# Reordering pair 0's second-half scores, two exponentials and the last output rows in a fused attention and feed-forward kernel

## The chip, the cores and the metric

The kernel runs on one core of a Trainium2 chip. The metric is device time in microseconds (us). Before the change five runs gave a median of 241.13 us (241.03 to 241.76).

## The reference

Two blocks follow each other. The first is windowed attention over `q, k, v` of shape (4 batches, 8 heads, 768 rows, 64 columns); each query sees the first 8 keys and its last 96 keys, and a slope per head times the distance is subtracted from the score:

```python
scores = scale * q @ k.T - slope[h] * dist      # masked outside the window
a = exp(scores - max) ; a = a / (sum(a) + 1e-9)
x = (a @ v)            # laid out as 3072 tokens x 512
```

The second is a gated feed-forward block with a hidden width of 1536:

```python
g = x @ w_gate
out = ((g * sigmoid(g)) * (x @ w_val)) @ w_out   # 3072 x 512, float32
```

## The kernel before

**Tiles.** The 3072 tokens are cut into 8 tiles of 384; tile 0 is the first half of batch 0, tile 1 its second half, and so on. For each tile the hidden width is cut into 12 slices of 128. One slice is a gate product (4 matmuls of 384 columns into the PSUM tile `gps`), a value product (4 matmuls into `vps`), a tanh on ScalarE (`th`, L564), a combination on VectorE (`sl`, L569) and a multiplication on VectorE (`hT`, L573), which is the activated slice in 16 bits. A block of 128 output rows is 12 matmuls of 512 columns into `ops` (L585), an evacuation on ScalarE (`osb`, L591) and a write by SyncE's DMA queue (L592). The very last block of 128 rows has its own function, `out_last`.

**Attention around it.** Heads are worked in four pairs per batch. For batch 0 the two halves of 384 rows are worked apart. A pair's second half needs: transposes of its keys and queries on TensorE (`turn_half`, L298, into `trs`), copies of these out of PSUM into `kT` (three copies of 96, 240 and 48 columns, L319) and into `qT` (one copy of 384 columns, L336), a bias product that writes slope times distance (`bias`, L345, into four `sc` banks), the scores that add to it (`scores_half`, L356), and exponentials on ScalarE (L367): two of 264 columns for which = 0 and two of 432 columns for which = 1. Denominators and numerators follow (L445).

**PSUM.** There are eight banks with fixed names. `a0` to `a3` go round for scores, bias and numerators; the first four gates of tile 0 stand in them too. `o0` holds an output block, or transposes. `x0`, `x1`, `x2` go round for the gates and values (`spare`), so that each of these waits for the reader of the one three places before it. Gate 4 stands in `x1`, gate 5 in `x2`, value 4 in `x0`, value 5 in `x1`, gate 6 in `x2`: gate 6 can start when gate 5 has been read by its `sl`.

**Order.** Nothing is scheduled automatically; every engine works its instructions in the order in which the code emits them, so the order of the calls is the order on each engine, and semaphores alone hold an engine back. For tile 0 this order is the list `tile0` (L802). A pair (f, 0) is gate f, (f, 1) is value f; other entries are attention steps. The gates 0 to 3 are multiplied ahead of the list, and `first_val(0)`, `first_val(1)` multiply the first two of four terms of values 0 and 1, so that (0, 1) and (1, 1) multiply the last two terms. `trh(h0, h1, ...)` turns and copies two pairs, `bias_of(0, w)` and `scores_of(0)` are pair 0's bias and scores, and `sch(hp)` is bias and scores of another pair in one step.

A list `later` holds work that is put off: `scores_half` with `put_off` appends its two exponentials of 432 columns to it instead of emitting them. The loop over `tile0` (L865) calls `run_later(1)`, which takes one entry, ahead of each gate or value except (8, 1):

```python
if item != (8, 1):
    run_later(1)
gate_or_val(0, f, which, ...)      # products, then tanh and sl, or hT
```

So an entry that is waiting is emitted on ScalarE ahead of the tanh of the gate that takes it.

**The DMA queues** of GpSimd bring the weights, the next batch's keys, queries and values in the meantime; the issues are in program order too, and their place is the same before and after. SyncE's queue writes outputs; of the last block, one half is written from SyncE's queue and the other from ScalarE's.

Of the kernel before, what the change touches and what calls it, by code (L numbers as in the profile page):

```python
# [37 lines left out]
def kernel(  # L38
# [12 lines left out]
    nc = tc.nc  # L51
# [7 lines left out]
    DM = H * D  # L59
# [5 lines left out]
    TB = 384  # L65
# [174 lines left out]
    def spare(name, dt=FP32):  # L240
        tag = state["x"][gv.get("n", 0) % len(state["x"])]
        gv["n"] = gv.get("n", 0) + 1
        return single(name, tag, dt)

    def single(name, tag, dt=FP32):
        return ps.tile([128, 512 if dt == FP32 else 1024], dt, name=name, tag=tag)
# [8 lines left out]
    def run_later(n):  # L255
        for _ in range(n):
            if later:
                later.pop(0)()
# [285 lines left out]
    def products(t, f, which, c0, c1, dst=None):  # L544
        if f == 0 and which == 0 and c0 == 0:
            hTs[t] = sb2.tile([128, NFF, TB], FP16, name="hT", tag="hT", bufs=3)
        if c0 == 0:
            if dst is None:
                dst = spare("gv"[which] + "ps")
            gv[f, which] = dst  # L550
        w = (wg, wv)[which]
        for c in range(c0, c1):
            nc.tensor.matmul(  # L553
                gv[f, which][:, 0:TB], lhsT=w[:, c, 128 * f:128 * f + 128],
                rhs=x_of(t)[:, c, :],
                start=(c == 0), stop=(c == NC - 1))

    def gate_or_val(t, f, which, c0=0):
        products(t, f, which, c0, NC)
        dst = gv.pop((f, which))  # L560

        if which == 0:
            th = sb2.tile([128, TB], FP32, name="th", tag="th")
            nc.scalar.activation(out=th, in_=dst[:, 0:TB], func=AF.Tanh, scale=0.5)  # L564
            if t == 0 and f < 4:
                sl = sb2.tile([128, TB], FP32, name="sl", tag="ns", bufs=4)
            else:
                sl = sb2.tile([128, TB], FP32, name="sl", tag="sl")
            nc.vector.scalar_tensor_tensor(  # L569
                out=sl, in0=th, scalar=1.0, in1=dst[:, 0:TB], op0=AluOp.add, op1=AluOp.mult)  # L570
            gv["sl", f] = sl
        else:
            nc.vector.tensor_mul(hTs[t][:, f, :], dst[:, 0:TB], gv.pop(("sl", f)))  # L573
# [18 lines left out]
            nc.sync.dma_start(out=out[r0:r0 + 128, :], in_=osb)  # L592

    def out_last(t, i):
        r0, n = TB * t + 128 * i, DM // 2
        for side, (ev, dq) in enumerate(((nc.vector.tensor_scalar_mul, nc.sync),
                                         (nc.scalar.mul, nc.scalar))):
            ops = single("ops", f"a{i + side}")
            c0 = n * side
            for f in range(NFF):  # L600
                nc.tensor.matmul(  # L601
                    ops[:, 0:n], lhsT=hTs[t][:, f, 128 * i:128 * i + 128],
                    rhs=wo[:, f, c0:c0 + n], start=(f == 0), stop=(f == NFF - 1))
            osb = sb2.tile([128, n], FP32, name="osb", tag="th")
            ev(osb, ops[:, 0:n], 0.5)
            dq.dma_start(out=out[r0:r0 + 128, c0:c0 + n], in_=osb)

    NT = TOK // TB
    pairs = {(b, hp): Pair(b, hp) for b in range(B) for hp in range(NP)}
# [30 lines left out]
    V, A = nc.vector.tensor_copy, nc.scalar.copy  # L640
# [64 lines left out]
    def first_gates(*terms):  # L705
        for c, f in terms:
            products(0, f, 0, c, c + 1, hb[f])
# [20 lines left out]
    def vas(b, half):  # L728
        return lambda: both_values(b, half)
# [1 line left out]
    def tr(b, hp):  # L731
        return pairs[b, hp].transposes

    def trh(h0, h1, last):
        def step():
            b0, b1 = single("trs", "o0", FP16), spare("trs", FP16)
            (a, b), (c, d) = [(t[:, 0:TB], t[:, TB:2 * TB]) for t in (b0, b1)]
            pair_of = [(h0, (c, a)), (h1, (d, b))]
            for hp, tr in pair_of:
                pairs[0, hp].turn_half(1, tr)  # L740
            for hp, tr in pair_of:
                pairs[0, hp].copy_half(1, tr, V, A if hp == h0 else last)
        return step

    def sch(hp):
        def step():
            p = pairs[0, hp]
            scs = [p.bias(1, 0), p.bias(1, 1)]
            for which in range(2):
                p.scores_half(1, which, scs[which], which == 1 and hp != 1)  # L750
        return step
# [32 lines left out]
    def bias_of(hp, which):  # L784
        def step():
            pairs[0, hp].sc[1, which] = pairs[0, hp].bias(1, which)
        return step

    def scores_of(hp):
        def step():  # L790
            for which in range(2):
                pairs[0, hp].scores_half(1, which, pairs[0, hp].sc[1, which], which == 1)
        return step

    def first_val(f):
        return lambda: products(0, f, 1, 0, 2)
# [2 lines left out]
    V(out=dist[:, 2 * WIN + 168:], in_=dist[:, WIN:WIN + 48])  # L799
    first_gates(*[(c, f) for f in range(4) for c in range(2)])  # L800
    first_gates((2, 0), (2, 1), (2, 2), (3, 0), (3, 1), (2, 3), (3, 2), (3, 3))
    tile0 = [(0, 0), (1, 0), (2, 0), (3, 0), trh(0, 1, A), first_val(0), first_val(1),  # L802
             bias_of(0, 0), bias_of(0, 1), (0, 1), (1, 1), scores_of(0), (2, 1),
             trh(2, 3, V), sch(1), (3, 1), (4, 0), sch(2), (5, 0), (4, 1), (5, 1),
             (6, 0), (6, 1), sch(3), (7, 0), (7, 1), (8, 0), vas(0, 1), (8, 1)]

    def ff(t, f0, f1, n_out=(0,)):
# [22 lines left out]
    for b, base, rate, v_at in ((2, 20, 2.0, (31, 32, 33, 34, 35, 36, 37)), (3, 38, 1.4, (56, 57, 58, 59, 60, 61, 62))):  # L830
        items = [(base, lambda b=b: stage_rows(b)), (base + 1, lambda b=b: load_ends(b))]
        n = 0
# [27 lines left out]
    def take(step_list):  # L860
        run_later(len(later))
        for step in step_list:
            step()

    for item in tile0:  # L865
        if callable(item):
            take([item])
            continue
        f, which = item
        if item != (8, 1):  # L870
            run_later(1)
        gate_or_val(0, f, which, (NC if f < 4 else 0, 2 if f < 2 else 0)[which])
        for fn in after.pop((0, f, which), []):
            fn()
# [22 lines left out]
    for i in range(2):  # L897
        for part in range(4):
            out_part(NT - 1, i, part)
    out_last(NT - 1, 2)  # L900


# [33 lines left out]
```

## Time and profile before

The profile shows one execution, which took 241.76 us; its span, from the first to the last instruction, is 240.0 us, so 1.76 us lie around the span.

| what | value |
|---|---|
| median of 5 runs | 241.13 us |
| profiled execution | 241.76 us |
| its span | 240.0 us |
| TensorE (PE) busy | 233.1 us, 97% |
| VectorE (DVE) busy | 167.4 us, 70% |
| ScalarE (ACT) busy | 127.6 us, 53% |
| GpSimd (POOL) busy | 94.0 us, 39% |
| granted TensorE clock | 1.000 |
| four matmuls of 384 columns, in the chain | 0.65 us |
| the last block's 24 matmuls, in the chain | 2.63 us |

A row of the timeline has the start in us from the span's start, the length in us, the engine, the line of the code, the operation, what it writes and reads, the shapes and a count, for several merged instructions of the same kind; in brackets stands idle time of the engine ahead of it and what ended it. The end of a matmul is modelled, so a matmul's row lasts longer than the step to the next one; the step is read from the starts. PEld is the loading of weights, which goes on beside PE.

### The profile page before, as it was taken

The numbers are of one execution on the slowest core, as the hardware profiler recorded it, in microseconds if no ns is written. First come the engines' busy times: TensorE is split into PE (matmuls) and PEld (weight loads), VectorE is DVE, ScalarE is ACT, GpSimd is POOL, SyncE is SP. The second block draws the span as 40 slices with busy tenths as digits, with TensorE's granted clock in tenths as the row PEclk, the third lists the DMA queues.
The fourth block names the chain that finished last, engine by engine and source line by source line (L and its number), as shares of the span: only waits on it lengthen the run. The fifth ranks groups of instructions, "written<-read, shape, count | busy, mean of one in ns | idle before, by whom it ended". The sixth has DMA issues, their size and how long they took to land.

```text
span 240.0 us, 6040 instructions
## 1 busy us (share of the span) xinstructions
PE 233.1 (97%) x2424; PEld 135.6 (57%) x2424; DVE 167.4 (70%) x365; ACT 127.6 (53%) x288; POOL 94.0 (39%) x113
## 2 busy tenths in 40 slices
PE   7799999999999999999999999999999999999994
PEld 4555565656555556555655556555655556555543
DVE  6689559978897678776785668776785668555520
ACT  4747675888856365376356365376356435233311
POOL 8986673668970002994072152700031213000000
PEclk9999999999999999999999999999999999999999
DMA  7999999999998537999139849930110110111022
GB/s 134 158 200 201 181 203 205 196 165 159 156 137 125 122 82 120 117 131 122 44 62 109 117 109 133 120 61 0 48 44 3 44 44 3 46 45 44 12 79 87
DMA packets 83332, 25.00 MB, mean 104 GB/s; under 512 B 72600, under 2 KB 80360, under 8 KB 83304
## 3 DMA queue, kind: packets, MB, share of 16 engines
q0 software_dynamic: 64208, 14.05, 64.0%
q1 hardware_dynamic: 18664, 10.29, 17.7%
q8 instruction: 19, 0.31, 0.5%
q10 hardware_dynamic: 432, 0.27, 0.4%
q14 instruction: 9, 0.07, 0.1%
HBM read 28.62 MB, written 6.29 MB: 145 GB/s over the span
## 4 chain that ended last, share of the span: by engine, by line
PE 91%; ACT 3%; DVE 2%; DMA 2%; issue 1%; POOL 0%; DVEq 0%; ACTq 0%; POOLq 0%
PE gps L553 26%; PE vps L553 26%; PE ops L585 25%; PE num L445 4%; PE sc L385 3%; PE den L445 2%; DMA q<-in_q_dram 2%; ACT at L367 1%; PE sc L345 1%; PE trs L272 1%; DVE sl L569 1%; PE ops L601 1%; PE sc L356 1%; ACT th L564 1%; PE trs L298 1%; DVE xT L503 1%
## 5 line engine op out<-in xcount | busy, mean ns | idle before, releaser
L564 ACT ACTIVATE th<-gps 128x384 f32<-128x384 f32 x96 | 47.4, 495 | 63.2 <-PE gps L553 57.2
L569 DVE SCALAR_TENSOR_TENSOR sl<-th,gps 128x384 f32<-128x384 f32 x96 | 52.7, 550 | 38.9 <-ACT th L564 38.3
L553 PE MATMUL gps<-xT,wg 128*128 128x384 f16 x384 | 78.0, 327 | 0.7 <-DVE sl L569 0.3
L553 PE MATMUL vps<-xT,wv 128*128 128x384 f16 x384 | 78.0, 326 | 0.0
L585 PE MATMUL ops<-wo,hT 128*128 128x512 f16 x276 | 73.1, 379 | 0.0
L573 DVE TENSOR_TENSOR hT<-vps,sl 128x384 f16<-128x384 f32 x96 | 52.9, 553 | 8.1 <-PE vps L553 0.3
L553 PEld LDWEIGHTS <-wg 128*128 128x128 f16 x384 | 35.6, 98 | 32.2 <-issue 2.7
L553 PEld LDWEIGHTS <-wv 128*128 128x128 f16 x384 | 37.2, 98 | 25.5 <-issue 0.4
L585 PEld LDWEIGHTS <-hT 128*128 128x128 f16 x276 | 26.9, 98 | 23.6
L393 ACT ACTIVATE at<-sc 128x432 f16<-128x432 f32 x72 | 33.8, 533 | 10.2 <-PE sc L385 10.2
L522 POOL TENSOR_TENSOR xT<-ns,rb 128x384 f16<-128x384 f32 x10 | 9.8, 995 | 66.4 <-DVE rb L461 55.5
L169 POOL DMA_DIRECT2D vS<-in_v_dram x28 | 24.7, 899 | 4.9 <-DMA kst<-in_k_dram 1.7
L591 ACT ACTIVATE osb<-ops 128x512 f32<-128x512 f32 x23 | 13.7, 597 | 14.6 <-PE ops L585 14.4
L404 POOL TENSOR_TENSOR at<-at,masks 128x864 f16<-128x864 f16 x4 | 7.3, 1822 | 23.9 <-ACT at L393 19.3
L404 DVE TENSOR_TENSOR at<-at,masks 128x864 f16<-128x864 f16 x20 | 12.2, 609 | 5.6 <-ACT at L393 5.6
L518 ACT COPY ns<-num 128x384 f32<-128x384 f32 x24 | 9.8, 493 | 9.6 <-PE num L445 9.6
L192 POOL DMA_DIRECT2D kst<-in_k_dram x16 | 14.0, 897 | 2.0 <-PE sc L385 1.2
L192 POOL DMA_DIRECT2D qst<-in_q_dram x16 | 13.8, 890 | 0.2 <-issue 0.2
L367 ACT ACTIVATE at<-sc 128x432 f16<-128x432 f32 (+2 forms) x32 | 11.3, 461 | 3.3 <-PE sc L356 3.3
L401 DVE TENSOR_TENSOR at<-at,masks 128x432 f16<-128x432 f16 x24 | 8.1, 377 | 4.4 <-ACT at L393 4.4
L445 PE MATMUL num<-at,vS 128*32 128x216 f16 (+6 forms) x576 | 10.9, 224 | 0.0
L455 DVE STREAM_TRANSPOSE dT<-den 128x384 f32<-128x384 f32 x16 | 9.3, 580 | 1.1 <-PE den L445 0.4
(70 smaller groups left out, 164.7 us busy)
## 6 DMA issues: line engine op xcount, KB each, us to landing
out_dram<-osb SPq DMA_DIRECT2D x23, 256.0 KB
vS<-in_v_dram POOLq DMA_DIRECT2D x24, 120.0 KB, 5.7
wg<-in_moe_w_gate_dram POOLq DMA_DIRECT2D x6, 256.0 KB, 7.7
wv<-in_moe_w_val_dram POOLq DMA_DIRECT2D x6, 256.0 KB, 7.6
wo<-in_moe_w_out_dram POOLq DMA_DIRECT2D x4, 384.0 KB, 11.2
qst<-in_q_dram POOLq DMA_DIRECT2D x16, 96.0 KB, 5.1
kst<-in_k_dram POOLq DMA_DIRECT2D x16, 90.0 KB, 4.9
kst<-in_k_dram POOLq DMA_DIRECT2D x2, 384.0 KB, 12.7
```

Of the source, the lines that this page charges most:

```text
L169: nc.gpsimd.dma_start(out=vSs[b][NG:NG + n, c, :, :], in_=v[b, :, KC * c:KC * c + n, :].rearrange("h p d -> p h d"))
L192: nc.gpsimd.dma_start(out=st[b][p0:p0 + n, h // 2, :, h % 2, :], in_=src[b, h, 0:n * J].rearrange("(t p) d -> p t d", p=n))
L367: nc.scalar.activation(out=at[:, hi, 0:col + n], in_=sc[hi][:, 0:col + n], func=AF.Exp, scale=scale)
L393: nc.scalar.activation(out=at[:, hi, :], in_=sc[hi][:, 0:BANK], func=AF.Exp, scale=scale)
L404: mul_eng.tensor_mul(at, at, m[:, :, o:o + BANK])
L445: nc.tensor.matmul(dst[r, o:o + n], lhsT=ones[:, 0:32] if side is None else vals[:, 4 * g + j, side::2], rhs=pairs[b, 2 * g + j // 2].at[c ...
L553: nc.tensor.matmul(gv[f, which][:, 0:TB], lhsT=w[:, c, 128 * f:128 * f + 128], rhs=x_of(t)[:, c, :], start=(c == 0), stop=(c == NC - 1))
L564: nc.scalar.activation(out=th, in_=dst[:, 0:TB], func=AF.Tanh, scale=0.5)
L569: nc.vector.scalar_tensor_tensor(out=sl, in0=th, scalar=1.0, in1=dst[:, 0:TB], op0=AluOp.add, op1=AluOp.mult)
L573: nc.vector.tensor_mul(hTs[t][:, f, :], dst[:, 0:TB], gv.pop(("sl", f)))
L585: nc.tensor.matmul(ops, lhsT=hTs[t][:, f, 128 * i:128 * i + 128], rhs=wo[:, f, :], start=(f == 0), stop=(f == NFF - 1))
L591: nc.scalar.mul(out=osb, in_=ops, mul=0.5)
```

## The change

Three things change.

1. In `tile0`, `scores_of(0)` stands ahead of (0, 1) and (1, 1), the last two terms of values 0 and 1. With it, the copies of the first two pairs go by pair: pair 0's keys and queries are transposed into `o0` and all four copies are on ScalarE; pair 1's go into the other bank and all four copies are on VectorE. Before, the keys of both pairs stood in `o0` and were copied by VectorE (six copies), and the queries of both stood in the other bank and were copied by ScalarE (two copies). Pairs 2 and 3 keep that way.
2. The loop doesn't call `run_later` ahead of gate 5, (5, 0). Pair 2's two exponentials of 432 columns then stand behind gate 5's tanh on ScalarE, ahead of value 4, and no longer in front of that tanh.
3. In `out_last` the last 128 rows are worked in pieces of 384 and 128 columns instead of 256 and 256. VectorE evacuates the first piece, which SyncE's queue writes; ScalarE evacuates the second, which its own queue writes.

The order on TensorE changes in two places only: ten scores matmuls move ahead of four matmuls of the values, and the last 24 matmuls have other widths. The numbers of TensorE's instructions and of DMA issues are the same.

```diff
     def out_last(t, i):
-        r0, n = TB * t + 128 * i, DM // 2
-        for side, (ev, dq) in enumerate(((nc.vector.tensor_scalar_mul, nc.sync),
-                                         (nc.scalar.mul, nc.scalar))):
+        r0 = TB * t + 128 * i
+        for side, (c0, n, ev, dq) in enumerate((
+                (0, 384, nc.vector.tensor_scalar_mul, nc.sync),
+                (384, 128, nc.scalar.mul, nc.scalar))):
             ops = single("ops", f"a{i + side}")
-            c0 = n * side
             for f in range(NFF):
...
-    def trh(h0, h1, last):
+    def trh(h0, h1, by_pair):
         def step():
             b0, b1 = single("trs", "o0", FP16), spare("trs", FP16)
             (a, b), (c, d) = [(t[:, 0:TB], t[:, TB:2 * TB]) for t in (b0, b1)]
-            pair_of = [(h0, (c, a)), (h1, (d, b))]
-            for hp, tr in pair_of:
+            if by_pair:
+                jobs = [(h0, (b, a), A, A), (h1, (d, c), V, V)]
+            else:
+                jobs = [(h0, (c, a), V, A), (h1, (d, b), V, V)]
+            for hp, tr, _, _ in jobs:
                 pairs[0, hp].turn_half(1, tr)
-            for hp, tr in pair_of:
-                pairs[0, hp].copy_half(1, tr, V, A if hp == h0 else last)
+            for hp, tr, k_eng, q_eng in jobs:
+                pairs[0, hp].copy_half(1, tr, k_eng, q_eng)
         return step
...
-    tile0 = [(0, 0), (1, 0), (2, 0), (3, 0), trh(0, 1, A), first_val(0), first_val(1),
-             bias_of(0, 0), bias_of(0, 1), (0, 1), (1, 1), scores_of(0), (2, 1),
-             trh(2, 3, V), sch(1), (3, 1), (4, 0), sch(2), (5, 0), (4, 1), (5, 1),
+    tile0 = [(0, 0), (1, 0), (2, 0), (3, 0), trh(0, 1, True), first_val(0), first_val(1),
+             bias_of(0, 0), bias_of(0, 1), scores_of(0), (0, 1), (1, 1), (2, 1),
+             trh(2, 3, False), sch(1), (3, 1), (4, 0), sch(2), (5, 0), (4, 1), (5, 1),
              (6, 0), (6, 1), sch(3), (7, 0), (7, 1), (8, 0), vas(0, 1), (8, 1)]
...
         f, which = item
-        if item != (8, 1):
+        if item not in ((5, 0), (8, 1)):
             run_later(1)
```

## The prediction

> **What bounds the kernel now.** I read the page first, then TensorE's waits, then the chain of work that ended last, then the timeline around each place that the change touches.
>
> ```profile
> PE 233.1 (97%) x2424; PEld 135.6 (57%) x2424; DVE 167.4 (70%) x365; ACT 127.6 (53%) x288; POOL 94.0 (39%) x113
> ...
> PE 91%; ACT 3%; DVE 2%; DMA 2%; issue 1%; POOL 0%; DVEq 0%; ACTq 0%; POOLq 0%
> ```
>
> TensorE is busy nearly everywhere (97% of the span), and 91% of the chain is its own. Work on other engines therefore counts only where TensorE stands still for it. TensorE's waits name the places:
>
> ```profile
> PE warm L621 <- DVE ones L126: 1.2, 1, 1.2
> PE trs L298 <- ACT at L367: 0.7, 1, 0.7
> PE trs L298 <- DMA k<-in_k_dram: 0.7, 2, 0.4
> PE gps L553 <- DVE sl L569: 0.3, 1, 0.3
> PE gps L553 <- DVE xT L503: 0.3, 1, 0.3
> ```
>
> Of these only the fourth, a gate waiting for an `sl`, lies in the part that is changed. The timeline shows how it comes about (TensorE, ScalarE, VectorE, from 26.7 us):
>
> ```profile
> 26.73 1.52 ACT L367 ACTIVATE at<-sc 128x264 f16<-128x264 f32 x4 [0.32 <-PE sc L356]
> 26.81 0.82 PE L553 MATMUL gps<-xT,wg 128*128 128x384 f16 x4
> 27.47 1.46 PE L553 MATMUL vps<-xT,wv 128*128 128x384 f16 x8
> 28.10 0.53 ACT L564 ACTIVATE th<-gps 128x384 f32<-128x384 f32 x1
> 28.66 0.55 DVE L569 SCALAR_TENSOR_TENSOR sl<-th,gps 128x384 f32<-128x384 f32 x1 [1.67 <-ACT th L564]
> 29.27 0.81 PE L553 MATMUL gps<-xT,wg 128*128 128x384 f16 x4 [0.33 <-DVE sl L569]
> ```
>
> Gate 5 (26.81) has been issued by 27.47, but its tanh starts at 28.10 because pair 2's four exponentials are in front. Gate 6 needs gate 5's bank and starts at 29.27. After it no wait of TensorE is listed, so whatever is won here reaches the end.
>
> **Gate 5's tanh ahead of two exponentials.** The earliest tanh: gate 4 is followed by the next matmul at 25.71 and its tanh starts at 25.91, so the way from TensorE to ScalarE takes 0.20; gate 5's tanh can start at 27.47 + 0.20 = 27.67. ScalarE is free: of the four exponentials the two of 264 columns stay in front, and the third started at 27.28. Then tanh 0.49 (the row of L564) to 28.16, 0.03 to VectorE, `sl` 0.55 to 28.74, 0.06 to TensorE (28.66 + 0.55 to 29.27): gate 6 can start at 28.80. Values 4 and 5 end at 27.47 + 2 x 0.65 = 28.77, so 0.03 of the wait is left. Gain 29.27 - 28.80 = **0.47 us**. The list of waits says 0.3 because a matmul's modelled end hides the rest.
>
> The two exponentials of 432 columns now queue behind that tanh, from about 28.06 to 29.02 (the two lasted 0.96 together before). Who waits for them: pair 3's bias, whose third and fourth banks they free, at about 30.3 by the new count, and gate 6's tanh behind them, at 29.45 + 0.20 = 29.65. Both have over half a us; this costs nothing.
>
> A gain can be eaten by a load, since DMA isn't faster. Issue plus time to landing against the new moment of use: gate 8's weights 24.49 + 7.7 = 32.2 against 32.8; value 8's 27.25 + 7.6 = 34.9 against 35.5; the second part of `wo` 29.1 + 11.0 = 40.1 against 40.4; the queries of the next batch 31.56 + 13.8 = 45.4 against 46.0. All hold, the third by 0.3 only. These stalls could take at most the gain back.
>
> **Pair 0's scores ahead of the values, and the copies by pair.**
>
> ```profile
> 18.82 0.95 ACT L564 ACTIVATE th<-gps 128x384 f32<-128x384 f32 x2 [0.30 <-DVE sl L569]
> 19.64 1.12 PE L345 MATMUL sc<-dist,slopeI 128*128 128x72 f16 x6
> 19.66 0.86 ACT L336 COPY qT<-trs 128x384 f16<-128x384 f16 x2
> 20.27 1.27 DVE L319 COPY kT<-trs 128x96 f16<-128x96 f16 x6
> 20.59 0.81 PE L553 MATMUL vps<-xT,wv 128*128 128x384 f16 x4
> 21.34 0.48 PE L356 MATMUL sc<-qT,kT 64*128 64x72 f16 x10
> ```
>
> Bias ends at 20.59 (its last matmul waits until 20.41 for the fourth gate's `sl`). From full matmuls to the half-height scores there is a step of about 0.10 (four values from 20.59 end at 21.24, scores at 21.34). So scores can start at 20.69 if pair 0's keys and queries are there. ScalarE has four copies from 19.66 on. Two of 384 columns started 0.36 apart, though each lasts 0.48; by columns (384 less some 0.04 of start, 0.83 ns each) those of 96, 240 and 48 take about 0.12, 0.24, 0.09, and the last of 384 ends 0.49 after its start: 19.66 + 0.45 + 0.49 = 20.60, and with 0.04 to TensorE 20.64. That is in time by 0.05: cost **0**. Ceiling, with no overlap: 0.26 + 0.38 + 0.22 + 0.48 = 1.34, ready at 21.04, a stall of 0.35. I take 0, since the overlap stands in the ScalarE row itself.
>
> Otherwise it is an exchange: the same matmuls, and the same two changes of height. Scores 20.69 to 21.10, values to 21.75, where value 2 starts now too. A gain isn't to be had either, since the bias waits for the same `sl` as before. VectorE drops three key copies and gets one query copy: three copies 0.60, then 0.55, to about 21.42, where six took until 21.55. Value 0 ends at 21.42, so its `hT` starts at 21.62, later by 0.16, and the third `hT` waits for value 2 at 22.61 as before; pair 2's key copies start when they did. The transposes for pairs 2 and 3 need value 0's bank, read by 22.17, at 22.69. Pair 0's exponentials run earlier, and nothing waits for them that early. This part alone: 0.
>
> **Last rows in 384 and 128.**
>
> ```profile
> 12.72 0.20 PEld L345 LDWEIGHTS <-slopeI 128*128 128x128 f16 x4 [0.18 <-issue]
> 235.46 0.42 DVE L605 TENSOR_SCALAR osb<-ops 128x256 f32<-128x256 f32 x1 [5.43 <-PE ops L601]
> 236.77 0.38 ACT L605 ACTIVATE osb<-ops 128x256 f32<-128x256 f32 x1 [1.97 <-PE ops L601]
> 237.19 0.37 ACTq L606 DMA_DIRECT2D out_dram<-osb  x1
> ```
>
> TensorE: 12 x 0.1625 + 12 x 0.054 (128 columns at the 0.423 ns of the 384s) = 2.60 against 2.63 in the chain: equal, if a load of 128 columns of weights fits beside a matmul of 54 ns. The load row: four loads in 0.20, each about 0.10 long, so three steps take 0.10, 33 ns each: it fits. A rule speaks against it: the Trainium skill, "TensorE: Matmul & The Clock Gate", section "Back-to-back issue gap", gives about 81 ns for each pair of load and matmul at 128 columns. By it the piece takes 12 x 0.081 = 0.97, or 0.32 more. The row is of this kernel, so I take 54; the 98 ns that one load lasts, taken serially, would be the ceiling (+0.53).
>
> Second evacuation: 384 columns take 0.49 and 256 take 0.38 on ScalarE, so 128 take 0.28: 0.10 earlier. The write: on the old path 0.87 lay between the issue at 237.19 and the first data at 238.06; data lasted until 238.58, and 1.40 follows to the end (two stretches: their limits, their length, each engine's busy time, the clock, the DMA engines' busy share, GB/s):
>
> ```profile
> 238.05:238.58 0.53, 0.00 (x0) 0.00 (x0) 0.00 (x0) 0.00 (x0) 0.00 (x0) 1.00 0.73 247
> 238.58:239.98 1.40, 0.00 (x0) 0.00 (x0) 0.00 (x0) 0.00 (x0) 0.00 (x0) 1.00 0.00 0
> ```
>
> A block of 256 KB before took 0.83 and 128 KB 0.53, so by a straight line 64 KB take 0.38 and 192 KB 0.68. New second write: issue 237.09, data 237.96 to 238.34 alone. The first write is now later: matmuls end 0.63 later, VectorE takes 0.13 longer (0.55 for 384), issue 236.68, data from 237.51 to 238.19. They overlap for 0.23. The skill's "DMA: Bandwidth & Descriptors", section "Queues, rings and completion order", says that SyncE's and ScalarE's queues share the same 16 engines, taken in turn; no run here shows two such writes together. Fully shared, both end at 237.51 + 0.68 + 0.38 = 238.57. Between 238.34 and 238.57, against 238.58 before: 0.01 to 0.24 gained; I take the middle, **0.13**, rounded up to 0.15 because neither write kept the engines over three quarters busy (0.73).
>
> **Sum.** -0.47 + 0 - 0.15 = -0.62. Against the profiled execution: span 240.0 to 239.4, and its 1.76 around unchanged. The median is another execution, 0.63 below the profiled one, with the same work; the difference carries over: 241.13 - 0.62 = 240.5.
>
> **Rivals.** About 0.2% (0.48 us) is what a measurement of this kernel can tell from no change.
>
> *A, as worked out*: 240.5; own range 240.3 to 240.75.
>
> *B, the tail gives nothing or loses.* Loads pace the narrow matmuls or the two writes collide. By the 81 ns: evacuation ends at 237.37, data at 238.65, +0.07; serial loads +0.28. For it the page's rule, against it the load row. -0.47 + 0.07 to +0.28: 240.7 to 240.95.
>
> *C, the wait moves.* Pair 0's copies take ScalarE to their ceiling (0.35), or a load lands late behind gate 6 (`wo` has 0.3). For it the small margins, against it the overlap seen in the copies. -0.62 + 0.35: about 240.85.
>
> *D, slower: ScalarE's copies become the bound.* Scores now stand in front of values that would have hidden them; TensorE can't pass them. It decides from a stall of 0.62, copies of 1.6 us. If each of the four cost as much as an exponential of 432 columns, 0.55, without overlap, they would end at 21.86 and the stall be 1.21: 241.13 - 0.62 + 1.21 = 241.7. Against it: a ScalarE copy of 720 columns into `kT` lasts 0.77 and one of 48 lasts 0.22.
>
> **Numbers.** A 0.57, B 0.18, C 0.17, D 0.08. Faster by over 0.2% means below 240.65: nine tenths of A and a little of B and C, 0.55. D is slower except at its edge, 0.07; the rest, 0.38, is within. Range: A's lower end with a whole tail gain, 240.2, to past B and C, 241.0; D and the edges are left out.
>
> **What would show it.** Right: TensorE's list of waits without the gate's wait for `sl`, gate 6 starting some 0.03 after value 5 near 28.8, pair 0's scores near 20.7, narrow matmuls stepping by about 54 ns, last data near 238.0 (all earlier by the 0.47). Wrong: a wait of `sc` for a ScalarE copy at 20.7, a wait for a DMA between 30 and 46, a step of 80 ns or more in the last 12 matmuls, or both last writes ending together late.

## The result, and the profile after

| | before | after |
|---|---|---|
| median | 241.08 us (80 runs, 240.57 to 243.49) | 240.80 us (43 runs, 240.15 to 241.61) |
| profiled execution | 241.76 us | 241.21 us |
| its span | 240.0 us | 239.4 us |

Compared with runs of the kernel before on the same chips, the ratio is 0.9982, with a 95% interval of 0.9974 to 0.9990: faster by 0.43 us (0.24 to 0.63). The medians of the table, over all chips together, differ by less, 0.28 us. The forecast was 0.62 faster, 240.5 us. The gain is clear of zero, but its middle lies just inside 0.2% (0.48 us), while the outcome that was given most of the chance (0.55) was a gain of more than that.

In the profile's page of the kernel after, the first line is the busy time of each engine and the second the share of each in the chain that ended last:

```profile
PE 233.0 (97%) x2424; PEld 135.1 (56%) x2424; DVE 167.8 (70%) x363; ACT 127.7 (53%) x290; POOL 93.9 (39%) x113
...
PE 92%; DMA 3%; DVE 2%; POOL 1%; ACT 1%; issue 0%; DVEq 0%; ACTq 0%; POOLq 0%
```

TensorE's busy time has hardly changed (233.0 after 233.1), so what was won is time in which it stood still. In the list of its waits the gate's wait for an `sl` (L569) is gone, and no wait of the scores for a ScalarE copy has come in its place:

```profile
PE warm L621 <- DVE ones L126: 1.2, 1, 1.2
PE trs L298 <- ACT at L367: 0.9, 1, 0.9
PE trs L298 <- DMA q<-in_q_dram: 0.8, 2, 0.7
PE gps L553 <- DVE xT L503: 0.3, 1, 0.3
```

The timeline of the kernel after around gate 6 shows the first step at work:

```profile
26.77 0.67 ACT L367 ACTIVATE at<-sc 128x264 f16<-128x264 f32 x2 [0.32 <-PE sc L356]
26.86 0.82 PE L553 MATMUL gps<-xT,wg 128*128 128x384 f16 x4
27.52 1.46 PE L553 MATMUL vps<-xT,wv 128*128 128x384 f16 x8
27.72 0.49 ACT L564 ACTIVATE th<-gps 128x384 f32<-128x384 f32 x1 [0.28 <-PE gps L553]
28.11 0.95 ACT L367 ACTIVATE at<-sc 128x432 f16<-128x432 f32 x2
28.24 0.55 DVE L569 SCALAR_TENSOR_TENSOR sl<-th,gps 128x384 f32<-128x384 f32 x1 [1.21 <-ACT th L564]
28.85 0.81 PE L553 MATMUL gps<-xT,wg 128*128 128x384 f16 x4
```

The tanh (L564) starts at 27.72, which is 0.20 after gate 5 was issued, and it is ahead of the two exponentials of 432 columns (28.11). Gate 6 starts at 28.85 instead of 29.27, 1.33 after value 4: two values of 0.65 and 0.03 of wait.

The same view around pair 0's scores (the lines that answer those of L345, L336, L319, L553 and L356 before):

```profile
19.67 1.12 PE L345 MATMUL sc<-dist,slopeI 128*128 128x72 f16 x6
19.70 0.60 ACT L319 COPY kT<-trs 128x96 f16<-128x96 f16 x3
20.15 0.53 ACT L336 COPY qT<-trs 128x384 f16<-128x384 f16 x1
20.31 0.68 DVE L319 COPY kT<-trs 128x96 f16<-128x96 f16 x3
20.73 0.48 PE L356 MATMUL sc<-qT,kT 64*128 64x72 f16 x10
21.14 1.47 PE L553 MATMUL vps<-xT,wv 128*128 128x384 f16 x8
```

ScalarE's four copies go from 19.70 to 20.68 and the scores start at 20.73. All of this execution is 0.04 later than that of before, so this is 20.69 on the old count, the moment that was worked out. It was close: the step from the last bias matmul to the scores is 0.28 here and 0.27 further below, in the kernel whose copies are as before, so at most 0.01 of it is a wait for the last copy.

And the last rows, in the timeline of the kernel after:

```profile
233.53 2.78 PE L601 MATMUL ops<-wo,hT 128*128 128x384 f16 x24
235.68 0.56 DVE L605 TENSOR_SCALAR osb<-ops 128x384 f32<-128x384 f32 x1 [6.07 <-PE ops L601]
236.35 0.28 ACT L605 ACTIVATE osb<-ops 128x128 f32<-128x128 f32 x1 [1.97 <-PE ops L601]
236.66 0.37 ACTq L606 DMA_DIRECT2D out_dram<-osb  x1
```

with the stretches of the two writes and of what follows them (limits, length, busy time of each engine, clock, the DMA engines' busy share, GB/s):

```profile
237.10:237.72 0.62, 0.00 (x0) 0.00 (x0) 0.00 (x0) 0.00 (x0) 0.00 (x0) 1.00 0.98 342
237.63:237.97 0.34, 0.00 (x0) 0.00 (x0) 0.00 (x0) 0.00 (x0) 0.00 (x0) 1.00 0.81 228
238.00:239.43 1.43, 0.00 (x0) 0.00 (x0) 0.00 (x0) 0.00 (x0) 0.00 (x0) 1.00 0.00 0
```

The second evacuation takes 0.28, as read off. By the packets in the trace, data of the first piece (192 KB) move from 237.10 to 237.80, those of the second (64 KB) from 237.63 to 238.00, and the span ends 1.43 later.

To find where the time came from, I cut both traces at the starts of matmuls (us). "To value 2" goes from the last gate multiplied ahead (gate 3's last term) to value 2 and holds the scores' part; "to gate 6" goes from value 2 to gate 6; "tail" goes from the first of the last 24 matmuls to the end of the span.

| | first gate starts | to value 2 | to gate 6 | gate 6 to 8 | gate 8 to first output block | tail | span |
|---|---|---|---|---|---|---|---|
| before | 14.99 | 3.82 | 7.52 | 3.71 | 5.95 | 6.03 | 239.98 |
| after | 15.03 | 3.84 | 7.05 | 3.71 | 5.95 | 5.90 | 239.43 |

Everything not in the table is equal within 0.03. From the first gate to the end it is 224.99 and 224.40: −0.47 at gate 6, +0.02 at the scores, −0.13 in the tail, together −0.58, and 0.01 of rounding.

### The profile page after: what moved, and what is told of

It reads as the page before. It is cut to its first block, busy times and chain, and to the rows that moved or that the text cites. A ratio compares the mean times of both kernels' runs of the same rounds, so it can differ in the third digit from the quotient of the medians.

```text
span 239.4 us, 6040 instructions
## 1 busy us (share of the span) xinstructions
PE 233.0 (97%) x2424; PEld 135.1 (56%) x2424; DVE 167.8 (70%) x363; ACT 127.7 (53%) x290; POOL 93.9 (39%) x113
## 4 chain that ended last, share of the span: by engine, by line
PE 92%; DMA 3%; DVE 2%; POOL 1%; ACT 1%; issue 0%; DVEq 0%; ACTq 0%; POOLq 0%
PE gps L553 26%; PE vps L553 26%; PE ops L585 25%; PE num L445 4%; PE sc L385 3%; DMA q<-in_q_dram 3%; PE den L445 2%; PE sc L345 2%; PE trs L272 1%; PE ops L601 1%; PE sc L356 1%; POOL k L118 1%; DVE sl L569 1%; DVE xT L503 1%; PE trs L298 1%
## 5 line engine op out<-in xcount | busy, mean ns | idle before, releaser
L564 ACT ACTIVATE th<-gps 128x384 f32<-128x384 f32 x96 | 47.3, 494 | 62.7 <-PE gps L553 56.6
L569 DVE SCALAR_TENSOR_TENSOR sl<-th,gps 128x384 f32<-128x384 f32 x96 | 52.7, 550 | 38.4 <-ACT th L564 38.0
L553 PE MATMUL gps<-xT,wg 128*128 128x384 f16 x384 | 78.0, 327 | 0.3 <-DVE xT L503 0.3
L553 PE MATMUL vps<-xT,wv 128*128 128x384 f16 x384 | 77.8, 326 | 0.0
L553 PEld LDWEIGHTS <-wg 128*128 128x128 f16 x384 | 35.6, 98 | 31.7 <-issue 2.2
L553 PEld LDWEIGHTS <-wv 128*128 128x128 f16 x384 | 37.2, 98 | 25.2
```

The source lines that it names most:

```text
L553: nc.tensor.matmul(gv[f, which][:, 0:TB], lhsT=w[:, c, 128 * f:128 * f + 128], rhs=x_of(t)[:, c, :], start=(c == 0), stop=(c == NC - 1))
L569: nc.vector.scalar_tensor_tensor(out=sl, in0=th, scalar=1.0, in1=dst[:, 0:TB], op0=AluOp.add, op1=AluOp.mult)
```

## The experiments

The theory was that of the prediction: three separate steps, −0.47 at gate 6's bank, 0 at the scores, −0.15 in the tail, and loads that hold. Its rivals were that one step carries all, that the copies by pair do nothing, that narrow matmuls are paced by their weights, and that loads take the gain back. The last rival grew weightier once the timed gain (0.43) stood below that of the profiles (0.58). No kernel here leaves out any of the computation. The stretches are those of the table above; since the first gate starts anywhere between 13.56 and 15.03 us, spans are not compared.

**Each part alone.** The kernel before with one part of the change each. Only gate 5's tanh:

```diff
-        if item != (8, 1):
+        if item not in ((5, 0), (8, 1)):
```

> Of the three parts only the second: pair 2's two exponentials of 432 columns behind gate 5's tanh. My theory, that this part carries most of the gain: gate 6 starts near 28.80 in place of 29.27, every later matmul comes earlier by 0.47 us, the span is shorter by 0.47 and the time by about 0.2%. The rival, that the wait moves: gate 6 starts early, but a wait for a load or for a bank appears between 30 and 46 us and the last block of outputs starts less than 0.3 us earlier.

Measured: value 2 to gate 6 7.06 instead of 7.52, the other stretches of tile 0 within 0.02 of those of before. The first step gives 0.46 without the others. In this execution (first gate at 14.13) a load was late further on. Weight loads of the tanh-only kernel, at the next batch's transposes:

```profile
44.86 0.36 PEld L272 LDWEIGHTS <-kst 128*64 128x64 f16 x12 [0.32 <-issue]
45.43 0.36 PEld L272 LDWEIGHTS <-qst 128*64 128x64 f16 x12 [0.21 <-DMA qst<-in_q_dram]
```

The queries are taken 0.57 after the keys, where the same step on TensorE is 0.36 in the kernels before and after: 0.21 of the gain went to a load. From the first gate to the end it is 224.79, which is 0.20 less than before, where 0.46 had been won at gate 6. Timed: 240.74 us, ratio 0.9993 (0.9977 to 1.0008), which alone would not show a gain of 0.19%, nor exclude it.

Only the scores ahead and the copies by pair (the kernel after, with `if item != (8, 1):` and the old `out_last`):

> Of the three parts only the first: pair 0's scores ahead of the last terms of values 0 and 1, and copies by pair. My theory, an exchange without gain: scores start at 20.7, value 2 starts within 0.03 us of where it started before, the wait of gate 6 for gate 5's sl stays at its place, the span changes by less than 0.05. The rival, that ScalarE's four copies come late: TensorE waits for them at 20.7 and everything later moves back by up to 0.35 us. A second rival, that this part gives a gain of its own: gate 6 starts more than 0.1 us earlier.

Measured: value 2 to gate 6 7.56, so the wait stays. To value 2 it is 3.91 instead of 3.82. TensorE's waits in this kernel name both:

```profile
PE vps L553 <- DMA wv<-in_moe_w_val_dram: 0.4, 1, 0.4
...
PE gps L553 <- DVE sl L569: 0.2, 1, 0.2
```

The first terms of the values waited 0.4 for their weights; most of that was made up, since the bias behind them waits for the fourth gate's `sl` in any case. So the price of this part is better read in the kernel after, +0.02; nothing shows a gain from it, and a kernel with the two other parts alone was not run. Timed: 241.14 us, ratio 0.9995 (0.9976 to 1.0015).

Only the tail in 384 and 128 columns (the `out_last` of the diff):

> Of the three parts only the third: last rows in 384 and 128 columns. My theory: the 24 matmuls take as long as before (narrow ones step by 54 to 56 ns), the second evacuation takes 0.28 us in place of 0.38, its write ends earlier by 0.1 to 0.25, the span is shorter by about 0.15. The rival, that loads pace the narrow matmuls at about 81 ns: 0.3 us longer on TensorE and a span longer by about 0.1. A second rival, that the two writes collide: both end together and the span changes by less than 0.05.

Measured: tail 5.89, a gain of 0.14; gate 6 as before (7.52). The narrow matmuls step by 55 to 57 ns here and in the kernel after. Timed: 240.67 us, ratio 0.9984 (0.9974 to 0.9995). The first gate started at 13.57, and a load was late again, at gate 8 this time, in a kernel whose tile 0 is that of before. Weight loads of the tail-only kernel:

```profile
32.08 0.11 PEld L553 LDWEIGHTS <-wg 128*128 128x128 f16 x2 [0.43 <-DMA wg<-in_moe_w_gate_dram]
```

Gate 8's third matmul, the first one that needs the second half of that load, starts 367 ns after the second instead of 162: 0.20 lost. From the first gate to the end it is 225.07, no less than before. By the times, the tail (0.39 us, 0.12 to 0.63) would look worth more than gate 5's tanh (0.17), the opposite of the stretches; with intervals this wide the times can't rank the parts, and their sizes rest on the traces.

**Are the copies by pair needed?** The kernel after, with the copies as before and the scores still ahead:

```diff
-    tile0 = [(0, 0), (1, 0), (2, 0), (3, 0), trh(0, 1, True), first_val(0), first_val(1),
+    tile0 = [(0, 0), (1, 0), (2, 0), (3, 0), trh(0, 1, False), first_val(0), first_val(1),
...
-                jobs = [(h0, (c, a), V, A), (h1, (d, b), V, V)]
+                jobs = [(h0, (c, a), V, A), (h1, (d, b), V, A if h0 == 0 else V)]
```

> The changed kernel with all three parts, but with the copies of pairs 0 and 1 as before (keys of both on VectorE, queries of both on ScalarE). My theory, that the order of the scores costs nothing only because pair 0's keys are copied on ScalarE: VectorE starts its key copies at 20.3 and has pair 0's three done at about 20.98, so the scores start near 21.05 in place of 20.73, everything later is 0.32 us later than in the changed kernel, and the span is shorter than before by about 0.25 in place of 0.55. The rival, that the copies don't matter: as the changed kernel, shorter by about 0.55.

A stall of 0.32 was expected; it was 0.1. Timeline of this kernel:

```profile
18.34 0.86 ACT L336 COPY qT<-trs 128x384 f16<-128x384 f16 x2
...
18.95 1.27 DVE L319 COPY kT<-trs 128x96 f16<-128x96 f16 x6
19.36 0.57 PE L356 MATMUL sc<-qT,kT 64*128 64x72 f16 x10
19.87 1.47 PE L553 MATMUL vps<-xT,wv 128*128 128x384 f16 x8
```

The scores start at 19.36, while VectorE copies keys until 20.22. They do not even wait for all three of pair 0, which end at 19.63: the first four matmuls find their keys copied, and the fifth starts at 19.57, when the second copy has ended (19.52). The ten take 0.51 (19.36 to 19.87) where the kernel after takes 0.41 (20.73 to 21.14). The copies by pair are worth about 0.10; to value 2 it is 3.92 against 3.84. Timed: 240.45 us, ratio 0.9984 (0.9974 to 0.9995), not to be told from the kernel after. Again an early start (13.67) and again gate 8's third matmul late, by 0.23.

**Is it the bank that gate 6 waits for?** The kernel before, with gate 6 in another bank and the tanh left where it was (what comes behind gate 6 moves on by one bank in the round):

```diff
-                dst = spare("gv"[which] + "ps")
+                dst = single("gps", "o0") if (t, f, which) == (0, 6, 0) else spare("gv"[which] + "ps")
```

> The kernel before with one edit: tile 0's gate 6 stands in the free bank o0 and no longer waits for gate 5's sl; ScalarE's order is the old one. My theory, that the wait is for the bank that gate 5's late tanh holds: gate 6 follows value 5 at once, so from value 2 to gate 6 it is 7.03 us as in the changed kernel (7.05) and not 7.52, although gate 5's tanh is as late as before. The rival, that the late tanh itself costs time further on (its slice's hT, or gate 6's tanh behind it): a new wait after gate 6, and the first output block no earlier than before, counted from value 2.

Timeline of this kernel:

```profile
25.54 1.52 ACT L367 ACTIVATE at<-sc 128x264 f16<-128x264 f32 x4 [0.32 <-PE sc L356]
...
26.28 1.47 PE L553 MATMUL vps<-xT,wv 128*128 128x384 f16 x8
26.92 0.52 ACT L564 ACTIVATE th<-gps 128x384 f32<-128x384 f32 x1
27.59 0.81 PE L553 MATMUL gps<-xT,wg 128*128 128x384 f16 x4
```

All four exponentials are in front of the tanh (26.92), which is as late as before, 0.64 behind value 4's start. Gate 6 starts all the same 1.31 behind value 4, without a wait: value 2 to gate 6 is 7.07, and gate 6 to 8 stays at 3.71. So the late tanh cost time through gate 5's bank alone, and as far as gate 8 the 0.45 can be had either way. Then, in this execution, a load took most of it. Weight loads of this kernel at gate 8:

```profile
31.97 0.11 PEld L553 LDWEIGHTS <-wg 128*128 128x128 f16 x2 [0.57 <-DMA wg<-in_moe_w_gate_dram]
```

Its first gate had started at 13.56, and gate 8's third matmul was late by 0.35. Counted from value 2, the first output block starts only 0.09 earlier than before. Timed: 240.77 us, ratio 0.9987 (0.9968 to 1.0006).

**A fill for the bias's wait.** The bias waits for the fourth gate's `sl` both before and after. In the kernel after, the values' last terms were put between the two halves of the bias:

```diff
-             bias_of(0, 0), bias_of(0, 1), scores_of(0), (0, 1), (1, 1), (2, 1),
+             bias_of(0, 0), (0, 1), (1, 1), bias_of(0, 1), scores_of(0), (2, 1),
```

> The changed kernel with the last terms of values 0 and 1 between the two bias products of pair 0, where TensorE waits for the fourth gate's sl. My theory: the 0.28 us of that wait are filled, and value 2 starts about 0.29 us earlier from the last of gate 3's terms (3.55 against 3.84), held by VectorE's copy of pair 1's queries out of value 2's bank. Whether the 0.29 reach the end is the other question: if the loads bound this stretch, gate 8 or the transposes of the next batch's queries wait longer and part of it is lost; if they don't, the time is 0.1% below the changed kernel's.

Inconclusive: the values themselves waited. Timeline of this kernel:

```profile
19.86 0.82 PE L553 MATMUL vps<-xT,wv 128*128 128x384 f16 x4 [0.78 <-DMA wv<-in_moe_w_val_dram]
```

To value 2 it is 4.42 by this load. Timed: 240.57 us, ratio 0.9976 (0.9955 to 0.9996). With the same order and, in addition, gate 8's weights issued ahead of the last loads of `v`, the attention's values:

```diff
+    load_w(wg, 8)
     for c in range(3, NCH):
         load_v_rest(0, c)
-    load_w(wg, 8)
     load_w(wv, 8)
```

> As the run with the filled wait, and the last third of the gate weights is loaded ahead of the values of pair 0's second half. My theory, that loads bound gate 8 in executions that start early: the wait inside gate 8 is gone, so from gate 8 to the first output block it is 5.95 us in whatever execution (6.17 to 6.19 were seen where gate 8 waited); the wait at the next batch's queries can remain. The rival, that the longer step came from elsewhere (for instance from ScalarE): 6.1 or more is seen again.

```profile
19.03 0.39 PE L345 MATMUL sc<-dist,slopeI 128*128 128x72 f16 x4
19.26 0.81 PE L553 MATMUL vps<-xT,wv 128*128 128x384 f16 x4
19.91 0.53 PE L345 MATMUL sc<-dist,slopeI 128*128 128x432 f16 x2
20.37 0.48 PE L356 MATMUL sc<-qT,kT 64*128 64x72 f16 x10
```

In this timeline the values (19.26) lie between the halves of the bias and nothing waits: 3.55 to value 2, 0.29 less than the kernel after, as expected. Gate 8 did not wait, but the first gate started at 14.38, and at 14.30 and 14.48 gate 8 does not wait in other kernels either, so this run doesn't decide between its theory and the rival. Timed: 240.85 us, ratio 0.9988 (0.9969 to 1.0008): a gain of 0.29 in the profile did not appear in the times. Beside them the kernel after ran once more, unchanged:

> The changed kernel once more, beside the three others on one chip. My theory: from value 2 to gate 6 7.05 us, the last 24 matmuls to the end 5.90; the first gate's start is set by the first loads and can lie anywhere between 13.5 and 15.1; if it lies early, a wait for a load stands inside gate 8 or at the next batch's queries, and the span is not shorter by all of the early start. If loads have nothing to do with it, no such wait is seen at an early start.

Its stretches are 3.84, 7.05, 3.71, 5.95 and 5.90, the same as in its first trace; first gate to end 224.43. With a first gate at 14.48 it did not try an early start. Timed: 240.69 us, ratio 0.9976 (0.9957 to 0.9996).

**Does a late load take the gain?** The kernels before and after, both with gate 8's weights issued behind value 8's, so that gate 8 has to wait for them:

```diff
-    load_w(wg, 8)
     load_w(wv, 8)
+    load_w(wg, 8)
```

> The kernel before, with the last third of the gate weights loaded behind that of the value weights instead of ahead of it, so that it lands about 2.7 us later (near 34.9). My theory: gate 8 waits for it, from gate 8 to the first output block it takes about 7.5 us in place of 5.95, and the time grows by 1.5 to 2 us. It is the base for its twin with the change.

> The changed kernel with the same late load. My theory, that a bound load takes the gain: gate 6 starts 0.47 us sooner after value 2 as always (7.05), but gate 8 waits that much longer, so that from gate 3's last term to the first output block it is as long as in the twin without the change (within 0.2, the jitter of the load), and of the change only the 0.13 at the end are left. The rival, that the gain of the order on ScalarE reaches the end whatever the loads do: that stretch is 0.45 shorter than in the twin.

Timeline of the kernel before with the late load, at gate 8:

```profile
33.50 0.50 PE L553 MATMUL gps<-xT,wg 128*128 128x384 f16 x2 [0.76 <-DMA wg<-in_moe_w_gate_dram]
34.82 0.50 PE L553 MATMUL gps<-xT,wg 128*128 128x384 f16 x2 [0.82 <-DMA wg<-in_moe_w_gate_dram]
35.25 0.79 PE L445 MATMUL den<-at,ones 128*32 128x72 f16 x40
```

and of the kernel after with it:

```profile
33.58 0.50 PE L553 MATMUL gps<-xT,wg 128*128 128x384 f16 x2 [1.72 <-DMA wg<-in_moe_w_gate_dram]
34.84 0.74 PE L553 MATMUL gps<-xT,wg 128*128 128x384 f16 x2 [0.77 <-DMA wg<-in_moe_w_gate_dram]
35.51 1.35 PE L445 MATMUL den<-at,ones 128*32 128x72 f16 x40
```

In the first, gate 6 to gate 8 takes 4.63 and gate 8 to the first output block 6.95, together 1.92 longer than in the kernel before; a time longer by 1.5 to 2 had been expected. Gate 6 started at 29.92 in the first and at 29.04 in the second, 0.88 earlier (0.49 of it from the earlier first gate, the rest from the change). Gate 8's third matmul starts at 34.82 and 34.84. In this pair the landing did not move with TensorE's work: up to gate 8 the gain is gone entirely, waited off at 33.5 (1.72 instead of 0.76). From gate 3's last term to the first output block the two were expected equal within 0.2, and they were not: 25.02 against 22.92. Of these 2.10, some 0.5 is the earlier first gate, waited off as well; the rest lies behind gate 8 (8.48 against 6.95), where after the longer wait TensorE's granted clock fell. Stretches of the kernel after with the late load (columns as above; the third figure from the end is the clock):

```profile
33.50:35.50 2.00, 1.16 (x4) 0.23 (x4) 0.00 (x0) 0.00 (x0) 1.45 (x3) 0.87 1.24 208
35.50:37.00 1.50, 1.50 (x53) 1.44 (x56) 0.86 (x2) 0.77 (x2) 0.40 (x2) 0.50 1.24 205
37.00:38.80 1.80, 1.80 (x77) 1.64 (x69) 1.23 (x4) 1.13 (x3) 0.76 (x1) 0.62 1.26 207
```

Timed: 243.32 us, ratio 1.0097 (1.0064 to 1.0131), and 244.03 us, 1.0102 (1.0067 to 1.0136). The times are not told apart, but the intervals are too wide to exclude that 0.2% was kept, and three of the six executions of the second against one of the first have a lower mean clock (0.993). What shows the loss is the trace, one pair of executions.

**Gate 8's weights early, without the fill.** The kernel after with the edit of loads shown for the fill, and nothing else:

> The changed kernel with the last third of the gate weights loaded ahead of the values of pair 0's second half. My theory: no wait inside gate 8 at any start, otherwise the stretches of the changed kernel (3.84, 7.05, 5.95, 5.90); the median is at or a little under the changed kernel's, by at most 0.1%. The rival, that the values now land too late for the numerators: a wait near 33 to 34 us and a longer stretch from gate 8 to the first output block.

Gate 8's steps are 163, 162 and 163 ns, no wait. Value 8 waits in its place; its row in this timeline takes 1.10, where 0.81 is the rule:

```profile
35.02 1.10 PE L553 MATMUL vps<-xT,wv 128*128 128x384 f16 x4
```

In that execution the first terms also started 0.77 late, for want of their weights, so its stretches are longer than those of the kernel after (4.24 to value 2, 6.22 from gate 8 to the first output block). Timed: 240.49 us, ratio 0.9961 (0.9944 to 0.9977). This is the lowest ratio of all, at the edge of that of the kernel after (0.9974 to 0.9990). It is the best of many kernels, and the next one, which holds the same edit, gave 0.9980; so it isn't shown to be better. To relieve the first terms as well, the first value weights were split so that their first half lands sooner:

```diff
-    load_w(wv, 0)
+    load_w(wv, 0, 2)
...
+    load_w(wv, 2, 2)
```

(with `load_w` taking the number of slices, on top of the edit before).

> The changed kernel with the last third of the gate weights loaded ahead of the values, and with the first third of the value weights loaded in two steps, the columns of values 0 and 1 first. My theory, that the first terms of value 0 start late in some executions only because their load of 512 KB lands late: with half of it ahead, they start 1.05 us after gate 3's last term in any execution (1.31 to 1.82 were seen), and the time is at or under that of the run without the split. The rival: GpSimd's queue, which has two issues more, falls behind, a later load is late, and the time is longer.

Nothing waited in that execution: 3.84, 7.05, 3.71, 5.95. The kernel after shows the same without the split, so one execution can't tell what it is worth. Timed: 240.67 us, ratio 0.9980 (0.9962 to 0.9997).

## Why the prediction was right or wrong

*Gate 5's tanh, −0.47.* Right, in size and mechanism, as far as gate 6: −0.47 in both traces of the kernel after, −0.46 with this part alone, and −0.45 when the bank was changed in its place. "Whatever is won here reaches the end" held for some executions only (see below). The list of waits said 0.3 before; reading the step from the starts was right. The remaining wait of 0.03 is there too. The two exponentials that now queue behind the tanh (28.11 to 29.06) delayed nobody, since gate 6 to 8 stayed at 3.71.

*Scores ahead and copies by pair, 0.* Right to 0.02: 3.84 against 3.82. The choice between the overlapped copies (ready at 20.64) and the ceiling (21.04) fell on the right end: on the old count the last one ended at 20.64. With 0.04 to TensorE that is 20.68, where 20.64 had been forecast (the query copy took 0.53, not 0.49), so hardly anything was left of the margin of 0.05. Left out was that the scores wait copy by copy; so even the old copies would have cost only 0.10.

*The tail, −0.15.* It measured −0.13 to −0.14. The narrow matmuls step by 56 ns, where 54 had been read off. The load row that stood for this is an average: its four loads start 15, 65 and 28 ns apart, so it did not show that every load fits into 54. In the tail they do: each load lasts 98 ns and they start 56 apart. The 81 ns of the Trainium skill ("TensorE: Matmul & The Clock Gate", "Back-to-back issue gap") does not hold in this sequence, in which each narrow matmul has a fresh load of 128 columns of weights. By that rule the tail would have lost its gain. The writes cost each other little: the last data ended at 238.00. Gate 6's gain, the 0.02 of the scores and the later start (0.04) shift the old count by −0.41, so on that count it is 238.41, near the unshared 238.34 and further from the fully shared 238.57. The difference lies ahead of the data and not in them: the second write's data lasted 0.37, but came 0.97 after its issue, where they had come after 0.87 before. Whether the first write, then running, caused this is not shown. Shared engines ("DMA: Bandwidth & Descriptors", "Queues, rings and completion order") are no contradiction: the first write had 0.17 left to run when the second began.

*The sum, −0.62.* From the first gate to the end the profiles give −0.58, in the interval of the timed −0.43 (0.24 to 0.63), as is −0.62, at its edge.

*"All hold": the step that failed in part.* The margins of the loads were counted from one execution, whose first gate started at 14.99 and which was the slowest of five, and the gain was carried over to the median ("the same work"). Others start up to 1.43 earlier, while the landing of a load need not move with it. The three earliest starts (13.56, 13.57 and 13.67) all had gate 8 wait, by 0.35, 0.20 and 0.23, and one of 14.13 had the queries late by 0.21. For gate 8 a margin of 0.6 had been counted; between the landing and the matmul that uses it there were 0.31 in the first trace of the kernel after (32.57 and 32.88), and 0.11 in the second.

The nine traces whose loads are issued as in the kernels before and after allow an estimate (us). Behind value 2, gate 8's third matmul falls due after 11.56 in the old order and after 11.09 in the new one; at the earliest it starts 0.05 after the second half of its weights has landed. Each execution's own landing then tells how much of the 0.47 would be waited off at gate 8:

| | first gate | second half landed | wait seen at gate 8 | of the 0.47 it would lose |
|---|---|---|---|---|
| before | 14.99 | 32.20 | 0 | 0 |
| after | 15.03 | 32.57 | 0 | 0 |
| after, once more | 14.48 | 32.22 | 0 | 0 |
| tanh only | 14.13 | 31.94 | 0.01 | 0.02 |
| scores only | 14.30 | 32.59 | 0 | 0.41 |
| tail only | 13.57 | 32.04 | 0.20 | 0.47 |
| copies as before | 13.67 | 31.79 | 0.23 | 0.23 |
| gate 6 in `o0` | 13.56 | 31.93 | 0.35 | 0.38 |
| fill | 14.04 | 31.91 | 0 | 0 |

The mean loss is 0.17, which makes −0.41 of the −0.58, near the timed −0.43. This is an estimate from single executions of different kernels, with the other loads left out. The timed interval also covers −0.58, so it is not shown that loads are the whole difference; without it, the middle would have lain beyond 0.2%. "Could take at most the gain back" held at gate 8 in these nine; in the late-load pair the longer wait was followed by the lower clock, and more than the gain was lost.

*Rivals.* B (the tail gives nothing) and D (ScalarE's copies become the bound) did not occur. C (the wait moves) did not occur in either trace of the kernel after; its second half, a load that comes late, occurred in other kernels, at other places than `wo`, and with starts earlier than the one counted. The timed gain puts the result at 240.70 (241.13 − 0.43), near the upper end of A's own range (240.3 to 240.75). If the estimate above is right, it lies there because C's second half comes true in a part of the executions, which A had not counted.

## What to carry to other kernels

When a gain lies ahead of fixed loads, count the margin of each load from the earliest start and the latest landing that executions show, not from the profiled one; a gain larger than the margin is worth no more than the margin. A wait of an in-order engine for a bank is removed by freeing the bank sooner or by taking another one; swapping the two in an experiment tells whether the bank was what it waited for. And read a wait from the steps between starts: the list of waits said 0.3 for one that was worth 0.47.

## What the hardware showed that was not expected

- The first gate's start differed by up to 1.47 us between the profiled executions (13.56 to 15.03), before any work that the edits touch. In the nine executions of the table above it came 6.1 to 6.4 us after a load of keys had landed (issued at 2.90, landed between 7.12 and 8.92). First terms of the values waited for their weights in four of fourteen (0.26 to 0.77 longer than the usual 1.05).
- The weight loads from gate 8's on followed earlier loads and not TensorE: in all fourteen traces each of these four was issued 0.28 to 0.29 us after the load eight places before it, among GpSimd's, had landed (two of them 0.36 and 0.42 in the split kernel).
- After two waits of 1.72 and 0.77 us TensorE's granted clock was at half for 3.41 us (34.96 to 38.38), and the denominators took 1.35 instead of 0.79. After waits of 0.76 and 0.82, in the twin, it stayed full.
- Two writes that overlap at the end, 192 KB and 64 KB on two queues, took 0.70 and 0.37 us, where a straight line through single writes gave 0.68 and 0.38; 0.10 more lay between the second one's issue and its data than before.
